# Attention, soft mixture of experts and a feed-forward layer on one core: queries and keys loaded by the batch, value tails in a home of their own

## The chip, the cores and the metric

The kernel runs on one core of one Trainium2 chip. The metric is the device time of one execution in microseconds (us); the time of a kernel is the median of several executions. Five engines each work through a list of their own: TensorE (PE, matrix products; PEld is its loading of weights), VectorE (DVE), ScalarE (ACT), GpSimd (POOL) and SyncE (SP), which here does nothing but start DMAs. Sixteen DMA engines move the data.

## What is computed

```python
def _attn_ref(q, k, v):                    # q, k, v: 8 batches, 8 heads, 576 tokens, 64 wide, float32
    scores = scale * np.matmul(q, k.transpose(0, 1, 3, 2))
    mask = block_i >= block_j              # blocks of 64 tokens
    scores = np.where(mask, scores, -1000000000.0)
    attn = np.exp(scores - max); attn = attn / (sum + 1e-09)
    return np.matmul(attn, v)
x = attn_out, one row of 512 for each of the 4608 tokens
x = _moe_ref(x, phi, w1, w2)               # soft mixture of 8 experts, 4 slots each, inner width 1024
return _moe2_ref(x, w_in, w_out)           # relu(x @ w_in) squared, @ w_out; inner width 2048
```

The three stages run one after the other. The change lies in the attention, which fills the first 435 us or so.

## The kernel before

The attention works on pairs of heads: head j and head 4 + j of one batch are a pair, so there are 8 batches of 4 pairs, 32 pairs in all, numbered n = 4b + j. `pair(n)` (L957) writes out one step: the scores of pair n, the pass over the maxima of pair n + 2 (`maxpass`, L443), the product with the values of pair n - 1 (`pv`, L583), and the splitting of queries and keys of pair n + 3 into a high and a low fp16 part (`split`, L394). PE works in exactly the order in which this is written (`manual_schedule`). SP's order is not written by hand: a scheduler puts each DMA where its own simulation finds it ready, those written earlier first, and SP then starts them strictly one after the other. A DMA whose data are not ready holds up all that stand behind it. In the program every DMA also waits for the one that was started eight places before it (eight semaphores in rotation), so at most eight are on their way.

SP starts these DMAs in the attention:

- `load_pair(n)` (L322): the keys and the queries of a pair, two heads each. `main` (L326, the DMA at L328) loads 512 tokens of one head, 128 KB; `tail` (L333, the DMA at L335), once for each batch, loads the last 64 tokens of four heads, 64 KB. They go into `qk_tile(b)` (L120): batches take turns in two places, in `ar_lo` and in `ar_hi`. `pair(n)` loads pair n + 7 (`LOOK`, L917, L1006 to L1008), so 2 + 2 of these DMAs belong to each pair, and 4 tails to each batch.
- `load_v(n)` (L301): the values of a pair, two DMAs of 128 KB (L306) and two tails of 16 KB (L312), which lie in a fifth block of the pair's own tile (`v_tile`, L124, four tiles in turn).
- the transposing DMA at L426, which turns the split keys (`ka`) into `s1`. `maxpass` needs it in the next pair. It is called s1(n) in this text, for pair n.
- the transposing DMA at L512, which turns the split queries with the maxima (`qb`) into `t2`, needed by the scores of the pair: t2(n).
- `s2copy(n)` (L924), a copy of the upper half of s1(n) into one of two tiles `s2`, needed by the second matmul of the scores (L528) of pair n, and possible once the scores of pair n - 2 are done.
- `load_in` (L908), pieces of 512 KB of w_in (`raw`), and pieces of the experts' weights w1 (L165, L167): work for the stages behind, taken in ahead.

The scales of a pair need the sum of squares of its queries and keys (`scale`, L348, the squares at L354 on ACT); this is what first reads the loaded data.

The loads stand in a list `dq`, from which four are taken at each of the eight places of a pair (`LR`):

```python
if n + LOOK < N:
    at = len(dq) if n < 1 else 0
    dq[at:at] = {0: load_pair(6), 1: load_pair(7) + load_pair(8)}.get(n) or load_pair(n + LOOK)
```

Of the kernel before, what the change touches and what calls it, by code (L numbers as in the profile page):

```python
# [23 lines left out]
def tile_attn_soft_moe_ffn(  # L24
# [12 lines left out]
    nc = tc.nc  # L37
    B, H, S, D = q.shape
# [6 lines left out]
    NJ = H // 2  # L45
    NU = S // 128
# [36 lines left out]
    ar_hi = hi_p.tile([128, NHI * 512], F32, name="ar_hi")  # L83
# [6 lines left out]
    V0 = NHI - 5  # L90
# [29 lines left out]
    def qk_tile(b):  # L120
        t = (ar_lo, ar_hi[:, 9 * 512:18 * 512])[b % 2].rearrange("p (w x j d) -> p w x j d", w=2, j=NJ, d=D)
        return dict(q=t[:, 0], k=t[:, 1])

    def v_tile(n):  # L124
        c0 = 512 * V0 + 640 * (n % 4)
        return ar_hi[:, c0:c0 + 640].rearrange("p (a h d) -> p a h d", h=2, d=D)

    def wchunk(i):
        kind, g, c = wlist[i]
# [106 lines left out]
    def attention():  # L236
# [22 lines left out]
        N = B * NJ  # L259
# [41 lines left out]
        def load_v(n):  # L301
            b, j = divmod(n, NJ)
            t = v_tile(n)

            def main(hp):
                nc.sync.dma_start(  # L306
                    out=t[:, 0:NU, hp, :], in_=v[b][NJ * hp + j, 0:128 * NU, :].rearrange("(u p) d -> p u d", p=128)
                )

            def tail():  # L310
                for h in range(2):
                    nc.sync.dma_start(out=t[64 * h:64 * h + 64, NU, 0, :], in_=v[b][NJ * h + j, 128 * NU:S, :])  # L312

            return [lambda: main(0), tail, lambda: main(1)]

        def load_phi(hp):
            nc.sync.dma_start(
# [4 lines left out]
        def load_pair(n, by={}):  # L322
            b, j = divmod(n, NJ)
            t = qk_tile(b)

            def main(nm, hp):  # L326
                src = dict(q=q, k=k)[nm][b]
                by.get(nm, nc.sync).dma_start(  # L328
                    out=t[nm][:, hp:2 * NU:2, j, :],
                    in_=src[NJ * hp + j, 0:128 * NU, :].rearrange("(u p) d -> p u d", p=128),  # L330
                )

            def tail(nm, hp):  # L333
                src = dict(q=q, k=k)[nm][b]
                by.get(nm, nc.sync).dma_start(  # L335
                    out=t[nm][64 * hp:64 * hp + 64, 2 * NU],
                    in_=src[NJ * hp:NJ * hp + NJ, 128 * NU:S, :].rearrange("j i d -> i j d"),
                )

            fs = []  # L340
            for nm in "kq":
                for f in (tail, main) if j == 0 else (main,):
                    fs += [lambda f=f, nm=nm, hp=hp: f(nm, hp) for hp in range(2)]
            return fs

        sc = {}

# [235 lines left out]
        def pv(n):  # L583
            b, j = divmod(n, NJ)
            vs = v_tile(n)
            pp = P[n]
            box = {}
# [18 lines left out]
            def tl(t):  # L606
                if t == 0:
                    box["tl"] = ps_v.tile([128, 384], F32, tag="tl", name="tl")
                for hp in range(2):
                    b_, c_ = pp[hp, 1], pp[hp, 2]  # L610
                    r = (b_[:, 0:64], b_[:, 448:512], c_[:, 256:320], c_[:, 448:512], pp["d"][:, hp, :])[t]
                    nc.tensor.matmul(
                        box["tl"][64 * hp:64 * hp + 64, 320:384], vs[:, t, hp if t < NU else 0, :], r,
                        start=(t == 0), stop=False,
                    )

# [281 lines left out]
        def wchunks(k):  # L898
            i = nxt[0]
            nxt[0] += k  # L900
            return [f for x in range(i, i + k) for f in wchunk((0, 1, 4, 5, 2, 3)[x] if x < 6 else x)]
# [12 lines left out]
            a, c = i % KD, i // KD  # L914
            return decode(dec_p, tin[:, a, 512 * c:512 * c + 512], raws.pop(i), 512)

        AHEAD, LOOK, LR = 3, 7, 4  # L917
        dq = load_pair(0, dict(q=nc.scalar)) + load_pair(1, dict(q=nc.scalar)) + load_pair(2) + load_pair(3)

        def loads(k):  # L920
# [6 lines left out]
        with tc.manual_schedule(engines={mybir.EngineType.Activation}):  # L927
            c0, c1, c2 = [scale([i]) for i in range(3)]
# [12 lines left out]
            for f in m0[6:] + m0[:6] + [sp2[0], sp2[1], sp2[3]]:  # L941
                f()
        dq += load_v(0) + load_pair(4) + load_v(1) + load_pair(5) + [lambda hp=hp: load_phi(hp) for hp in range(2)]
        s3 = scale([AHEAD])
        m1 = maxpass(1)
# [8 lines left out]
        work, aux, decq, nraw = [], [], [], [0, 0]  # L954
        NRAW = KD * FF // 512
        ew = early = late_ = last = half = None
        def pair(n):  # L957
            nonlocal dq, work, aux, decq, ew, early, late_, last, half
            bn, jn = divmod(n, NJ)
            m = maxpass(n + 2) if n + 2 < N else []  # L960
            s = scores(n) if n < N else []
# [17 lines left out]
            elif jn == 3:  # L979
                if bn + 1 == B:  # L980
                    early, late_, last = batch(bn)
# [17 lines left out]
            if n == 6:  # L999
                ew = wchunks(2)  # L1000
            if n >= 7 and ew:
                dq.append(ew.pop(0))
            if n + 2 < N:
                at = len(dq) if n < 4 else 0
                dq[at:at] = load_v(n + 2)
            if n + LOOK < N:  # L1006
                at = len(dq) if n < 1 else 0
                dq[at:at] = {0: load_pair(6), 1: load_pair(7) + load_pair(8)}.get(n) or load_pair(n + LOOK)  # L1008
            if n == 1:
                aux += scale([4]) + scale([5])  # L1010
            if n == 2:
# [40 lines left out]
            if n == N - 1:  # L1052
                half = wchunk(14)
# [595 lines left out]
```

## Time and profile before

| | |
|---|---|
| median of 3 runs | 892.95 us (890.33 to 894.09) |
| the profiled execution | 890.13 us, of which its span (first to last instruction) is 888.1 us |
| PE busy in the span | 823.8 us (93%) |
| DVE, ACT, POOL busy | 691.9 us, 627.3 us, 248.5 us |
| mean granted TensorE clock | 0.981 |
| moved by DMA | 113.18 MB in 222,022 packets, 193,760 of them under 512 B |

How to read the views used below. In a timeline a row is: start, duration (both us), engine, line, operation, output <- input, number of instructions merged; in square brackets the idle time of the engine just before, and what ended it. For SP (SPq) the duration is that of starting the DMA, with any wait in it, not that of the transfer. In the table of stretches a row is: the stretch, its length, then for PE, PEld, DVE, ACT and POOL the busy time with the number of instructions, then the granted TensorE clock (1.00 is 2.4 GHz, 0.5 is 1.2 GHz), the mean busy share of the DMA engines, and GB/s. In the table of DMA issues a row ends with KB of each and the median us from start to landing. In the chain of waits a row is: start, us, what. The waits table gives who waited for what: us in total, times, longest.

### The profile page before, as it was taken

The page shows a single profiled execution, that of the slowest core. Times are in us where ns is not written, and L with a number is a line of the kernel's source. Part 1 is how long each engine was busy: PE and PEld are TensorE (multiplying, and loading weights), DVE is VectorE, ACT ScalarE, POOL GpSimd, SP SyncE. Part 2 cuts the span into 40 slices and gives each one's busy share as a digit, 9 for nine tenths or more (in the row PEclk, how much of TensorE's full clock was granted, in tenths as well). Part 3 has the DMA queues.
Part 4 walks back from the last instruction along what each step waited for, and adds up shares of the span by engine and source line. Part 5 has one row for each costly group of instructions (what it writes and reads, how often), then busy time and mean ns, then how long its engine had stood idle before and what let it go on. Part 6 is the DMA issues. An engine that isn't in the chain of part 4 may idle for free.

```text
span 888.1 us, 21999 instructions
## 1 busy us (share of the span) xinstructions
PE 823.8 (93%) x8788; PEld 612.4 (69%) x8788; DVE 691.9 (78%) x1600; ACT 627.3 (71%) x1012; POOL 248.5 (28%) x394
## 2 busy tenths in 40 slices
PE   2778999999999999979997799999999999999997
PEld 1445767676676767656532444789898988888886
DVE  5857789999999998963633899788778888888880
ACT  5467777787878786734212889987888888887770
POOL 0225747666575756573100000000000000000000
PEclk9889999999999999999999899999999999999999
DMA  8798899999997898495999500100100000000002
GB/s 165 148 167 150 166 183 191 207 177 202 173 192 165 181 151 188 97 260 188 314 388 386 210 0 1 49 25 25 42 31 25 25 24 25 25 25 24 25 25 48
DMA packets 222022, 113.18 MB, mean 127 GB/s; under 512 B 193760, under 2 KB 195808, under 8 KB 221920
## 3 DMA queue, kind: packets, MB, share of 16 engines
q1 hardware_dynamic: 219264, 111.12, 53.3%
q8 instruction: 69, 1.13, 0.5%
q10 hardware_dynamic: 2656, 0.66, 0.4%
q14 instruction: 33, 0.27, 0.1%
HBM read 78.71 MB, written 9.44 MB: 99 GB/s over the span
## 4 chain that ended last, share of the span: by engine, by line
PE 60%; DVE 10%; DMA 8%; POOL 8%; ACT 7%; issue 3%; SPq 2%; ACTq 0%; DVEq 0%
PE ps_y L1463 14%; PE ps_x L1463 9%; PE ps_z L1463 9%; PE xm L601 5%; PE po L1485 4%; POOL ss L571 4%; PE ps_hb L1427 3%; POOL ul L711 3%; DMA wch<-in_moe_w_dram 3%; PE ps_sc L528 3%; DVE pm L465 2%; DMA s<-s 2%; DMA s<-ka 2%; PE ps_h L1154 1%; PE ps_max L451 1%
## 5 line engine op out<-in xcount | busy, mean ns | idle before, releaser
L1463 PEld LDWEIGHTS <-ah 128*128 128x128 f16 x1792 | 170.4, 98 | 21.8
L566 ACT ACTIVATE p<-ps_sc,es 128x512 f32<-128x512 f32 x192 | 128.0, 692 | 40.1 <-PE ps_sc L528 25.8
L1396 DVE TENSOR_TENSOR al<-a,ah 128x1024 f16<-128x1024 f32 (+1 forms) x128 | 138.5, 1125 | 16.7 <-ACT ah L1450 15.3
L571 POOL TENSOR_TENSOR ss<-p 128x384 f32<-128x384 f32 (+1 forms) x128 | 92.8, 745 | 171.8 <-ACT p L566 171.7
L465 DVE TENSOR_REDUCE pm<-ps_max 128x4 f32<-128x512 f32 x160 | 107.1, 681 | 32.1 <-PE ps_max L459 32.0
L1450 ACT CAST ah<-a 128x1024 f16<-128x1024 f32 (+1 forms) x128 | 114.4, 936 | 15.0 <-DVE a L1396 13.6
L528 PE MATMUL ps_sc<-t,s 128*128 128x512 f16 (+3 forms) x512 | 107.1, 302 | 12.0 <-DMA s<-s 7.9
L1556 POOL TENSOR_TENSOR ot<-u,p 128x256 f32<-128x256 f32 x16 | 12.5, 782 | 374.8 <-DVE u L1527 339.4
L1463 PE MATMUL ps_y<-bh,ah 128*128 128x256 f16 x384 | 104.8, 273 | 0.0
L1463 PE MATMUL ps_y<-bl,ah 128*128 128x256 f16 x384 | 104.7, 273 | 0.0
L1463 PE MATMUL ps_y<-bh,al 128*128 128x256 f16 x384 | 104.7, 273 | 0.0
L571 POOL TENSOR_TENSOR ss<-ss,p 128x320 f32<-128x320 f32 (+1 forms) x128 | 98.1, 766 | 10.5 <-ACT p L566 1.4
L1318 ACT ACTIVATE r<-ps_hb,alpha 128x1024 f32<-128x1024 f32 x64 | 71.1, 1112 | 34.1 <-PE ps_hb L1427 33.4
L1463 PEld LDWEIGHTS <-al 128*128 128x128 f16 x896 | 87.6, 98 | 10.0
L601 PE MATMUL xm<-p,ar_hi 128*64 128x256 f32 (+3 forms) x512 | 91.6, 457 | 0.0
L1396 DVE TENSOR_TENSOR a<-a 128x256 f32<-128x256 f32 x192 | 76.2, 424 | 3.9
L1463 PE MATMUL ps_x<-bh,ah 128*128 128x256 f16 x256 | 70.1, 274 | 0.0
L1463 PE MATMUL ps_z<-bh,ah 128*128 128x256 f16 x256 | 69.9, 273 | 0.0
L1463 PE MATMUL ps_x<-bh,al 128*128 128x256 f16 x256 | 69.8, 273 | 0.0
L1463 PE MATMUL ps_z<-bl,ah 128*128 128x256 f16 x256 | 69.8, 273 | 0.0
L1463 PE MATMUL ps_x<-bl,ah 128*128 128x256 f16 x256 | 69.8, 273 | 0.0
L1463 PE MATMUL ps_z<-bh,al 128*128 128x256 f16 x256 | 69.8, 273 | 0.0
(255 smaller groups left out, 1846.5 us busy)
## 6 DMA issues: line engine op xcount, KB each, us to landing
wch<-in_moe_w_dram SPq DMA_DIRECT2D x18, 1024.0 KB, 11.1
ar_hi<-in_v_dram SPq DMA_DIRECT2D x64, 128.0 KB, 3.2
raw<-in_moe_w_in_dram SPq DMA_DIRECT2D x16, 512.0 KB, 4.9
out_dram<-ot SPq DMA_DIRECT2D x32, 256.0 KB, 2.2
ar_hi<-in_moe_w_dram SPq DMA_DIRECT2D x6, 1024.0 KB, 8.7
s<-s SPq DMA_DIRECT2D x32, 144.0 KB, 3.4
ar_lo<-in_k_dram SPq DMA_DIRECT2D x32, 128.0 KB, 3.6
ar_hi<-in_k_dram SPq DMA_DIRECT2D x32, 128.0 KB, 3.4
```

The costliest lines, as they stand in the source:

```text
L465: nc.vector.tensor_reduce(out=o, in_=i, axis=AX.X, op=ALU.max)
L528: nc.tensor.matmul(ps[:, c0:c0 + w].rearrange("p (s c) -> p s c", c=128), kk[:, 2 * t + hp, :], qq[:, 2 * u0 + hp:8:2, :], start=(c0 == 0 ...
L566: exps[:] = [nc.scalar.activation(out=pt, in_=ps, func=AF.Exp, scale=es[:, 0:1])]
L571: add = lambda o, x, y: nc.gpsimd.tensor_tensor(out=o, in0=x, in1=y, op=ALU.add)
L601: nc.tensor.matmul(box["xm"][64 * hp:64 * hp + 64, 128 * t:512], vs[:, t, hp, :], r, start=(t == 0), stop=(t == 3),)
L711: add = lambda o, x, y: nc.gpsimd.tensor_tensor(out=o, in0=x, in1=y, op=ALU.add)
L1318: nc.scalar.activation(out=r[:, c0:c1], in_=ps[:, c0:c1], func=AF.Relu, **kw)
L1396: sub = lambda o, a, b: nc.vector.tensor_tensor(out=o, in0=a, in1=b, op=ALU.subtract)
L1427: nc.tensor.matmul(ps[:, 512 * j + 256 * a:512 * j + 256 * a + 256], ws[:, 128 * f:128 * f + 128], ctt[:, c0:c0 + 256], start=True, stop=True,
L1450: nc.scalar.copy(v(hl[n % 2][0][:, 2 * kq:2 * kq + 2], s), v(a7[n, kq], s))
L1463: nc.tensor.matmul(acc[:, 0:HM], a[:, k], b[:, k], start=bool(first and k + j == 0), stop=(k == KH - 1 and j == 2), skip_group_check=not f ...
L1485: nc.tensor.matmul(pos[t], g[:, 512 * a + 128 * t:512 * a + 128 * t + 128], tt[:, c, a], start=(c == 0 and a == 0), stop=(c == KH - 1 and ...
```

## The change

Queries and keys of the batches 2 to 7 are no longer loaded pair by pair. A new `load_batch(b)` loads a whole batch: four DMAs for the keys and four for the queries, each of 128 tokens of all eight heads (256 KB, L356 of the changed kernel), and the same four tails (L362 there). It is called in the second pair of batch b - 2: the tails and the keys are put into the list there, the queries in the pair after. Before, the four pairs of a batch were put in one by one, from the second pair of batch b - 2 on. Batches 0 and 1 are loaded as they were.

The value tails of a whole batch (64 tokens of four heads, two DMAs of 64 KB, L315 there) are loaded with the batch's first pair into a place of their own; the four value tiles shrink to four blocks.

```diff
     def v_tile(n):
-        c0 = 512 * V0 + 640 * (n % 4)
-        return ar_hi[:, c0:c0 + 640].rearrange("p (a h d) -> p a h d", h=2, d=D)
+        c0 = 512 * (V0 + n % NJ)
+        return ar_hi[:, c0:c0 + 512].rearrange("p (a h d) -> p a h d", h=2, d=D)
+
+    def v_tail(b):
+        c0 = 512 * (V0 + NJ) + 256 * (b % 2)
+        return ar_hi[:, c0:c0 + 256].rearrange("p (j d) -> p j d", d=D)
...
-            def tail():
-                for h in range(2):
-                    nc.sync.dma_start(out=t[64 * h:64 * h + 64, NU, 0, :], in_=v[b][NJ * h + j, 128 * NU:S, :])
-
-            return [lambda: main(0), tail, lambda: main(1)]
+            def tail(hp):
+                nc.sync.dma_start(
+                    out=v_tail(b)[64 * hp:64 * hp + 64],
+                    in_=v[b][NJ * hp:NJ * hp + NJ, 128 * NU:S, :].rearrange("j i d -> i j d"),
+                )
+
+            return [lambda: main(0)] + [lambda hp=hp: tail(hp) for hp in range(2) if j == 0] + [lambda: main(1)]
...
+        def load_batch(b):
+            t = qk_tile(b)
+
+            def main(nm, u):
+                nc.sync.dma_start(
+                    out=t[nm][:, 2 * u:2 * u + 2].rearrange("p x j d -> p (x j) d"),
+                    in_=dict(q=q, k=k)[nm][b][:, 128 * u:128 * u + 128, :].rearrange("h p d -> p h d"),
+                )
+
+            def tail(nm, hp):
+                nc.sync.dma_start(
+                    out=t[nm][64 * hp:64 * hp + 64, 2 * NU],
+                    in_=dict(q=q, k=k)[nm][b][NJ * hp:NJ * hp + NJ, 128 * NU:S, :].rearrange("j i d -> i j d"),
+                )
+
+            return [
+                [lambda nm=nm, hp=hp: tail(nm, hp) for nm in "kq" for hp in range(2)],
+                [lambda u=u: main("k", u) for u in range(NU)],
+                [lambda u=u: main("q", u) for u in range(NU)],
+            ]
...
-                        box["tl"][64 * hp:64 * hp + 64, 320:384], vs[:, t, hp if t < NU else 0, :], r,
+                        box["tl"][64 * hp:64 * hp + 64, 320:384], vs[:, t, hp, :] if t < NU else v_tail(b)[:, j, :], r,
...
-            if n + LOOK < N:
-                at = len(dq) if n < 1 else 0
-                dq[at:at] = {0: load_pair(6), 1: load_pair(7) + load_pair(8)}.get(n) or load_pair(n + LOOK)
+            if n == 0:
+                dq += load_pair(6)
+            if n == 1:
+                dq[0:0] = load_pair(7)
+            if jn == 1 and bn + 2 < B:
+                bl = load_batch(bn + 2)
+                dq[len(load_pair(7)) if n == 1 else 0:0] = bl.pop(0) + bl.pop(0)
+            if jn == 2 and bl:
+                dq[0:0] = bl.pop(0)
```

PE's, ACT's and POOL's instructions stay in their order, and DVE's but for some ten in the first pairs. SP's list falls from 488 entries to 392 and is ordered anew. Three places of it, all on SP; in each the first piece is the kernel before and the second the change. `s_..` with `ka` is an s1, `t_..` with `qb` a t2, `s_0` or `s_1` with `s_..` an s2copy.

The first place lies in pairs 1 and 2, from t2(2) to s1(4) (`s_648` before, `s_644` now).

```order
L512 DMA_TRANSPOSE t_634<-qb_140 128x9x128
L328 DMA ar_hi<-in_q_dram 128x4x64
L328 DMA ar_hi<-in_k_dram 128x4x64 x2
L328 DMA ar_hi<-in_q_dram 128x4x64 x2
L335 DMA ar_lo<-in_k_dram 64x4x64 x2
L328 DMA ar_lo<-in_k_dram 128x4x64 x2
L924 DMA s_0_141<-s_347 64x1152
L335 DMA ar_lo<-in_q_dram 64x4x64 x2
L328 DMA ar_lo<-in_q_dram 128x4x64
L426 DMA_TRANSPOSE s_648<-ka 128x9x128
```

```order
L539 DMA_TRANSPOSE t_631<-qb_140 128x9x128
L334 DMA ar_hi<-in_k_dram 128x4x64 x2
L334 DMA ar_hi<-in_q_dram 128x4x64 x2
L362 DMA ar_lo<-in_k_dram 64x4x64 x2
L362 DMA ar_lo<-in_q_dram 64x4x64 x2
L951 DMA s_0_141<-s_347 64x1152
L356 DMA ar_lo<-in_k_dram 128x8x64 x3
L453 DMA_TRANSPOSE s_644<-ka 128x9x128
```

Thirteen DMAs stood between the two transposes, and now twelve do, three of them of 256 KB.

The second place lies in pairs 3 to 5: s2copy(4) is `s_0_141<-s_648`, now `s_0_141<-s_644`, and s1(6) is `s_1097`, now `s_1091`; `t_1282` and `t_1270` are t2(5).

```order
L512 DMA_TRANSPOSE t_1085<-qb_139 128x9x128
L328 DMA ar_lo<-in_q_dram 128x4x64 x2
L306 DMA ar_hi<-in_v_dram 128x4x64
L426 DMA_TRANSPOSE s_1097<-ka 128x9x128
L312 DMA ar_hi<-in_v_dram 64x64 x2
L306 DMA ar_hi<-in_v_dram 128x4x64
L924 DMA s_0_141<-s_648 64x1152
L328 DMA ar_lo<-in_k_dram 128x4x64 x2
L328 DMA ar_lo<-in_q_dram 128x4x64 x2
L306 DMA ar_hi<-in_v_dram 128x4x64
L512 DMA_TRANSPOSE t_1282<-qb_140 128x9x128
```

```order
L539 DMA_TRANSPOSE t_1079<-qb_139 128x9x128
L310 DMA ar_hi<-in_v_dram 128x4x64 x2
L951 DMA s_0_141<-s_644 64x1152
L935 DMA raw<-in_moe_w_in_dram 128x1024 x2
L453 DMA_TRANSPOSE s_1091<-ka 128x9x128
L310 DMA ar_hi<-in_v_dram 128x4x64 x2
L169 DMA ar_hi<-in_moe_w_dram 128x512 x6
L951 DMA s_1_142<-s_880 64x1152
L539 DMA_TRANSPOSE t_1270<-qb_140 128x9x128
L169 DMA ar_hi<-in_moe_w_dram 128x512 x2
```

s2copy(4) moves ahead of s1(6); two pieces of w_in stand between them, and eight pieces of w1 (256 KB each) around t2(5), which before came later and one by one.

The third place recurs in every batch from batch 2 on: the pieces run from t2(11) to the copies of pairs 11 and 12 (`s_1_142` and `s_0_141`), pair 11 being the last of batch 2.

```order
L512 DMA_TRANSPOSE t_2684<-qb_140 128x9x128
L924 DMA s_1_142<-s_2249 64x1152
L328 DMA ar_lo<-in_k_dram 128x4x64 x2
L426 DMA_TRANSPOSE s_2734<-ka 128x9x128
L908 DMA raw<-in_moe_w_in_dram 128x1024
L328 DMA ar_lo<-in_q_dram 128x4x64 x2
L306 DMA ar_hi<-in_v_dram 128x4x64
L312 DMA ar_hi<-in_v_dram 64x64 x2
L306 DMA ar_hi<-in_v_dram 128x4x64
L924 DMA s_0_141<-s_2459 64x1152
```

```order
L539 DMA_TRANSPOSE t_2650<-qb_140 128x9x128
L356 DMA ar_lo<-in_q_dram 128x8x64
L310 DMA ar_hi<-in_v_dram 128x4x64
L453 DMA_TRANSPOSE s_2700<-ka 128x9x128
L315 DMA ar_hi<-in_v_dram 64x4x64
L935 DMA raw<-in_moe_w_in_dram 128x1024
L315 DMA ar_hi<-in_v_dram 64x4x64
L310 DMA ar_hi<-in_v_dram 128x4x64
L951 DMA s_1_142<-s_2223 64x1152
```

s2copy(11) came before s1(13) (`s_2734`) and now comes behind it and behind four loads.

## Rows read from the trace of the kernel before

**Rows 1.** The page, busy time of the engines.

```profile
PE 823.8 (93%) x8788; PEld 612.4 (69%) x8788; DVE 691.9 (78%) x1600; ACT 627.3 (71%) x1012; POOL 248.5 (28%) x394
```

**Rows 2.** Table of stretches: two of the attention, a short one, one of the experts.

```profile
50.00:100.00 50.00, 41.28 (x578) 27.20 (x576) 32.82 (x99) 37.20 (x77) 21.21 (x30) 0.90 0.87 158
200.00:250.00 50.00, 48.59 (x673) 34.12 (x674) 46.96 (x124) 38.10 (x79) 32.86 (x53) 1.00 1.05 189
...
48.00:54.00 6.00, 3.71 (x47) 2.48 (x46) 5.37 (x20) 5.42 (x12) 3.83 (x7) 1.00 1.15 219
...
440.00:490.00 50.00, 42.81 (x415) 14.79 (x413) 20.80 (x85) 12.95 (x24) 0.00 (x0) 0.97 1.03 377
```

**Rows 3.** Timeline of PE, 55 to 87 us: pairs 2, 3 and 4.

```profile
55.09 0.39 PE L528 MATMUL ps_sc<-t,s 128*128 128x512 f16 x1 [1.07 <-DMA s<-s]
58.21 0.59 PE L451 MATMUL ps_max<-s,t 128*128 128x128 f16 x2 [2.73 <-DMA s<-ka]
...
59.33 1.95 PE L601 MATMUL xm<-p,ar_hi 128*64 128x512 f32 x4
...
63.64 0.67 PE L435 MATMUL ps_qT<-id,qa 128*64 128x128 f16 x18
...
71.20 1.06 PE L601 MATMUL xm<-p,ar_hi 128*64 128x512 f32 x4
...
73.97 0.67 PE L435 MATMUL ps_qT<-id,qa 128*64 128x128 f16 x18
...
81.72 0.39 PE L528 MATMUL ps_sc<-t,s 128*128 128x512 f16 x1 [1.07 <-DMA s<-s]
81.94 0.38 PE L451 MATMUL ps_max<-s,t 128*128 128x128 f16 x2
...
82.58 1.60 PE L601 MATMUL xm<-p,ar_hi 128*64 128x512 f32 x4
...
87.02 0.67 PE L435 MATMUL ps_qT<-id,qa 128*64 128x128 f16 x18
```

**Rows 4.** Timeline of SP, 43 to 82 us, with one row of DVE.

```profile
43.70 1.51 SPq L512 DMA_TRANSPOSE t<-qb  x1
...
51.55 0.91 DVE L419 SCALAR_TENSOR_TENSOR ka<-ar_hi,sig,ka 128x576 f16<-128x576 f32 x1
...
54.27 1.42 SPq L426 DMA_TRANSPOSE s<-ka  x1
...
75.33 1.54 SPq L426 DMA_TRANSPOSE s<-ka  x1
...
78.83 0.51 SPq L924 DMA_DIRECT2D s<-s  x1
```

**Rows 5.** DMA issues of the whole run, by line and size.

```profile
ar_hi<-in_v_dram SPq DMA_DIRECT2D x64, 128.0 KB, 3.2
...
s<-s SPq DMA_DIRECT2D x32, 144.0 KB, 3.4
...
ar_hi<-in_v_dram SPq DMA_DIRECT2D x64, 16.0 KB, 3.3
...
s<-ka SPq DMA_TRANSPOSE x32, 4.3
```

**Rows 6.** Waits, 100 to 350 us: the longest of PE for a DMA.

```profile
PE ps_max L451 <- DMA s<-ka: 1.8, 1, 1.8
```

**Rows 7.** Timelines of SP, DVE and PE, 248 to 261 us, pair 18.

```profile
248.76 0.49 SPq L924 DMA_DIRECT2D s<-s  x1
...
252.55 0.87 DVE L419 SCALAR_TENSOR_TENSOR ka<-ar_hi,sig,ka 128x576 f16<-128x576 f32 x1
...
254.46 1.44 SPq L426 DMA_TRANSPOSE s<-ka  x1
...
260.62 0.59 PE L528 MATMUL ps_sc<-t,s 128*128 128x512 f16 x2
```

**Rows 8.** Chain of waits, 355 to 445 us: its longest step.

```profile
388.66 10.78 DMA s<-s
```

More of the change, by code (lines that the diff above doesn't have):

```diff
@@ L915, in decode_in @@
             return decode(dec_p, tin[:, a, 512 * c:512 * c + 512], raws.pop(i), 512)
-        AHEAD, LOOK, LR = 3, 7, 4
+        AHEAD, LR = 3, 4
         dq = load_pair(0, dict(q=nc.scalar)) + load_pair(1, dict(q=nc.scalar)) + load_pair(2) + load_pair(3)
@@ L956, in attention @@
         ew = early = late_ = last = half = None
+        bl = []
         def pair(n):
-            nonlocal dq, work, aux, decq, ew, early, late_, last, half
+            nonlocal dq, work, aux, decq, bl, ew, early, late_, last, half
             bn, jn = divmod(n, NJ)
```

## The prediction

> **What bounds the kernel now.** I read the page first, then the table of stretches, then the timelines of the stretches that stand out. PE is busy for 823.8 us of a span of 888.1 [rows 1], so 64 us are left, and a change of loads can only win where PE is idle or slowed. The stretches tell where that is [rows 2]. In the middle of the attention (200 to 250 us) PE is busy for 48.59 of 50 us at clock 1.00, and little is left to win. From 50 to 100 us it is busy for 41.28 us, at clock 0.90.
>
> The timeline of PE names what it waits for there [rows 3]: at 55.09 us 1.07 us for an s2copy, at 58.21 us 2.73 us for s1(4), at 81.72 us 1.07 us for s2copy(4). Each of these gaps is followed by a slow stretch: the work from the first value matmul to the transposes takes 4.31 us (59.33 to 63.64) after the first two and 4.44 us (82.58 to 87.02) after the third, against 2.77 us (71.20 to 73.97) at full clock. So the granted clock, fallen behind the gaps, costs another 1.54 and 1.67 us. All of it together, 1.07 + 2.73 + 1.07 + 1.54 + 1.67 = 8.1 us, is the most that better loads could win in the first pairs.
>
> The timeline of SP shows why two of these came late [rows 4]. The split keys of pair 4 were ready at 51.55 + 0.91 = 52.46 us, but SP started s1(4) at 54.27: it had been starting loads without a pause since t2(2) ended at 43.70 + 1.51 = 45.21, thirteen DMAs in 9.06 us, 0.70 us each. And s2copy(4) could go as soon as pair 2's scores were done, but stood behind s1(6), which was started at 75.33, and went at 78.83.
>
> **The change part by part.**
>
> *Fewer DMAs.* SP's list falls from 488 to 392 entries: 8 fewer loads of queries and keys in each of six batches, 6 fewer value tails in each of eight. At 0.70 us that is 67 us of SP's time, but SP is not on PE's path except where it is late. A tail of 16 KB lands after 3.3 us, a load of 128 KB after 3.2 [rows 5], so the small ones cost as much as the large. The Trainium skill says that transfers under 64 KB are mostly overhead and should be coalesced (DMA: Bandwidth & Descriptors, Rules for kernel authors); the rows agree. By that rule alone the sum would be nearer to the full 8.1 us. I don't take it, since the number of packets stays: each run of one head and one token is 256 B, before and after.
>
> *s1(4).* Between t2(2) and s1(4) stand twelve DMAs instead of thirteen, and ahead of t2(2) one fewer: two starts, 2 x 0.70 = 1.4 us earlier, which brings s1(4) from 54.27 to 52.9, just after its keys are ready. The twelve carry more: four loads of 128 KB, four of 64, a copy of 144 and three of 256, 1680 KB against 1424. They are started in 8.3 us, which asks for 207 GB/s; the same mix ran at 219 GB/s at 48 to 54 us [rows 2], so the queue holds. Bounds: nothing won (or 1.2 us lost, if the extra 256 KB stand in front at 219 GB/s), to 1.07 + 2.73 + 1.54 = 5.3 us if both gaps and the slow clock go. I take 1.4 us, nearest to the rows, with the slow clock left, as PE still waits over 1 us.
>
> *s2copy(4) and s1(6).* The copy now stands ahead of s1(6), so it starts at least 78.83 - 75.33 = 3.5 us earlier, and its gap of 1.07 us is gone. But two pieces of w_in, 1 MB, now stand between it and s1(6). At 377 GB/s, the rate of the long loads at 440 to 490 us [rows 2], they take 2.8 us. s1(6) was started at 75.33 and lands 4.3 us later [rows 5], at 79.6; PE asks for it at 81.94 [rows 3], and without the copy's gap at 80.9, so there is 1.3 us of room. The loads' 2.8 us use it up: PE then waits 1 to 1.5 us for s1(6) where it waited 1.07 us for the copy. I take 0, with bounds of 2.7 us won (gap and clock) and 2 us lost.
>
> *Eight pieces of w1 at once.* Six of them, 1.6 MB, stand ahead of t2(5) and s2copy(5): 4.2 us at 377 GB/s. In the kernel before these pieces came one by one. Both are needed only when pair 5 begins, and from pair 3 to pair 4 it is 11.4 us (71.20 to 82.58 [rows 3]); with 4.3 us to land, as s1 has, that leaves 2.9 us as cover, if t2(5) is ready as pair 4 begins. I take 0; without the cover up to 2 us are lost, and the clock with them.
>
> *The middle.* Each batch still moves the same bytes, with 14 fewer starts. PE waited 1.8 us in all for s1 between 100 and 350 us [rows 6]; half of it, 0.9 us, I count as won (bounds 0 and 1.8). Against that, the copy for the last pair of each batch moves behind s1 of the pair after next and four loads, 768 KB in all. In pair 18, for one: the keys are ready at 252.55 + 0.87 = 253.42 us, s1 then takes SP 1.44, the four loads 0.5 each (a copy's start took 0.49 there [rows 7]), 2.0 in all, and the copy lands 3.4 us after its start [rows 5]: 260.3 us. PE asks for it at 260.62. Before, it was started at 248.76. Its room shrinks to nothing, five times in a run (pairs 11 to 27). Bounds: 0 to 1.8 us for each time (768 KB at 219 GB/s are 3.6 us, of which SP's starts cover 2.0, and 0.2 for the room); I take 0.1, 0.5 us in all.
>
> *The end of the attention.* The copy that takes 10.78 us [rows 8], behind long loads of w1, keeps its place: 0. The value tiles' new places free no later than the old ones for the loads of w1: 0.
>
> **The sum.** 890.13 - 1.4 + 0 + 0 - 0.9 + 0.5 = 888.3 us for a run like the profiled one. The median of the runs shown lies 2.8 us above that execution; I add half of it, since a new median may lie anywhere between, and forecast **889.7 us**, about 2 us less than the kernel before on equal terms. A measurement of this kernel can tell about 0.5%, 4.5 us, from no change.
>
> **The rivals.**
>
> *The start comes free* (faster). SP's 96 fewer starts let every transpose and copy of pairs 2 to 5 go as soon as its data are ready, the three gaps close and the clock holds: 8.1 us at the start, 1.8 us in the middle less 0.5: 890.1 - 9.4 = 880.7 us; with half of the start, 885. For it: 0.70 us for each start in a stretch in which SP never paused, and gaps that all follow a late start. Against it: the loads of the start are moved earlier, 512 KB of keys more before s1(5), and w_in and w1 with them.
>
> *The copies come late* (slower). The DMAs are started in one line, and a small copy behind big loads waits for them: s2copy in rows 8 took 10.78 us instead of 3.4 [rows 5]. At the third place of SP's order the copy now has no room left, so anything over that, say 1 us for the 768 KB ahead of it in a stretch where the DMA engines' share is already 1.05 [rows 2], becomes a gap on PE in five batches, 5 us, and with the 2 us that pair 4 or 5 may lose 890.1 + 7 = 897 us. It decides from the point where the copy lands more than 7 us after the split keys are ready. The Trainium skill has the rule for it: on each DMA engine descriptors are consumed in ring order (DMA: Bandwidth & Descriptors, Queues, rings and completion order). Rows 8 agree. Against it: SP's own start times, 2.0 us for the four loads, already cover most of their transfer.
>
> *The loads themselves run faster* (faster). The new loads write 2 KB in one piece for each partition where the old ones wrote 256 B; if the write side set the rate, the start would be relieved of queue time as in the first rival: 882 us. No row shows a load whose rate tells the two sides apart.
>
> *The loads are hidden anyway* (no change). All of the terms are 0: 890 to 893 us. It is within the forecast's own range.
>
> **How the numbers follow.** The forecast, with no change as its edge: 0.45, from 885.5 to 894. The free start 0.30, of it most below 888. The late copies 0.20. Faster loads 0.05. So faster 0.35, within 0.5% 0.45, slower 0.20. Both outer cases hold much of the chance, so the range reaches from the full start, 881 us, to the late copies, 898 us; what lies beyond is at most 2 in 10.
>
> **What would show it.** In the profile of the changed kernel: s1(4) started at about 53 us and its gap on PE at 1 to 1.5 us instead of 2.73; the gap before pair 4 no longer on s2copy but on s1(6), about as long; busy PE in 50 to 100 us at 42 to 43 us; in the middle no wait for s2copy in the last pair of a batch. Wrong would be: PE idle for s2copy in pairs 11, 15, 19, 23 and 27 by more than 0.5 us each; a gap before pair 5; a clock of 1.00 from 50 to 100 us; or a change of the experts' stretch, which I count at 0.

## The result, and the profile after

The change makes the kernel slower: 904.86 us median of four executions (895.13 to 907.21) against 892.33 us of the kernel before beside it, a ratio of 1.0131 with a 95% interval of 1.009 to 1.0172. The forecast was 889.7 us with a range of 881 to 898: wrong in sign, and outside the range. The profiled execution took 904.28 us, its span 902.5 (before: 890.13 and 888.1). One execution of the runs below, 923.16 us of the run halves, was in a slower state and is left out of every number.

The page of the changed kernel, busy time of the engines (before: [rows 1]):

```profile
PE 829.6 (92%) x8788; PEld 613.8 (68%) x8788; DVE 692.9 (77%) x1600; ACT 627.9 (70%) x1012; POOL 248.4 (28%) x394
```

PE executes the same 8788 matmuls, and is busy 829.6 - 823.8 = 5.8 us longer for them. That is clock: the mean granted clock fell from 0.981 to 0.974, and 823.8 x 0.981 / 0.974 is 829.7. The span is 14.4 us longer, so the other 8.6 us are idle time. The table of stretches of the changed kernel tells where:

```profile
50.00:100.00 50.00, 37.06 (x461) 23.11 (x459) 29.71 (x90) 32.32 (x67) 19.53 (x28) 0.84 1.12 193
...
200.00:250.00 50.00, 46.51 (x643) 32.26 (x642) 44.23 (x115) 36.05 (x77) 30.13 (x47) 0.97 0.83 161
...
168.00:180.00 12.00, 8.46 (x63) 4.77 (x62) 11.76 (x29) 6.84 (x14) 7.08 (x10) 0.84 0.80 160
```

Against [rows 2], the first pairs lose 4.2 us of busy time and 2.1 us are lost from 200 to 250 us, which was full. The third row is a piece of 12 us around one gap: PE busy for 8.46 us, at a granted clock of 0.84, where the kernel before has 1.00 throughout the middle. The timeline of PE gives the gaps one by one (those over 0.6 us for a DMA, or for DVE behind one):

```profile
58.26 0.59 PE L478 MATMUL ps_max<-s,t 128*128 128x128 f16 x2 [2.56 <-DMA s<-ka]
...
72.75 0.39 PE L555 MATMUL ps_sc<-t,s 128*128 128x512 f16 x1 [2.12 <-DMA s<-s]
...
85.61 0.39 PE L478 MATMUL ps_max<-s,t 128*128 128x128 f16 x2 [0.66 <-DMA s<-ka]
...
97.72 0.59 PE L555 MATMUL ps_sc<-t,s 128*128 128x256 f16 x2 [3.96 <-DVE pm L492]
...
126.36 0.39 PE L555 MATMUL ps_sc<-t,s 128*128 128x512 f16 x1 [1.51 <-DMA s<-s]
...
176.78 0.61 PE L555 MATMUL ps_sc<-t,s 128*128 128x512 f16 x1 [2.65 <-DMA s<-s]
...
229.52 0.39 PE L555 MATMUL ps_sc<-t,s 128*128 128x512 f16 x1 [2.10 <-DMA s<-s]
...
280.40 0.39 PE L555 MATMUL ps_sc<-t,s 128*128 128x512 f16 x1 [1.90 <-DMA s<-s]
...
329.31 0.39 PE L555 MATMUL ps_sc<-t,s 128*128 128x512 f16 x1 [1.60 <-DMA s<-s]
...
352.82 0.39 PE L478 MATMUL ps_max<-s,t 128*128 128x128 f16 x2 [1.43 <-DMA s<-ka]
...
416.77 0.39 PE L555 MATMUL ps_sc<-t,s 128*128 128x512 f16 x1 [3.11 <-DMA s<-s]
```

The gap for s1(4) is as it was [rows 3]. New are the gap for s2copy(3) at 72.75, the one of 3.96 us before pair 5 at 97.72, and a row of five, at 126.36 to 329.31: they are the copies of pairs 7, 11, 15, 19 and 23, each the last pair of its batch. (Pair 27, also the last of one, has no gap over 0.3 us.) The waits of PE from 100 to 350 us sum them up:

```profile
PE ps_sc L555 <- DMA s<-s: 9.8, 5, 2.7
...
PE ps_max L478 <- DMA s<-ka: 0.9, 2, 0.5
```

In the kernel before, PE waited for the copies only once there, and 1.8 us for s1 [rows 6]:

```profile
PE ps_sc L528 <- DMA s<-s: 0.3, 1, 0.3
```

The shorter wait for s1 in this table is no gain. The 1.8 us are the wait for s1(27) at 333.49 us; in the change this wait comes at 352.82 us, 1.43 us long (the row above), just outside the stretch. With it PE waits 2.3 us for s1.

**The copy of the last pair of a batch.** SP's timeline of the changed kernel before the gap at 176.78 (pair 11):

```profile
166.57 1.78 SPq L453 DMA_TRANSPOSE s<-ka  x1
168.40 0.63 SPq L315 DMA_DIRECT2D ar_hi<-in_v_dram  x1
169.13 0.55 SPq L935 DMA_DIRECT2D raw<-in_moe_w_in_dram  x1
169.73 0.61 SPq L315 DMA_DIRECT2D ar_hi<-in_v_dram  x1
170.38 0.60 SPq L310 DMA_DIRECT2D ar_hi<-in_v_dram  x1
171.03 0.51 SPq L951 DMA_DIRECT2D s<-s  x1
```

and the step of the chain of waits that follows from its last row:

```profile
171.03 5.70 DMA s<-s
```

The copy is started 4.46 us after s1(13), behind 768 KB of loads, and lands 5.70 us after its start, at 176.73: PE goes on at 176.78. [Rows 5] have 3.4 us for this copy. By the chain of waits, the copies of pairs 15, 19 and 23 take 5.62, 5.40 and 5.03 us. Those of pairs 3 and 7 take 3.38 and 2.95, and no piece of w_in stands among the loads ahead of them: they are late by their start alone.

**The gap before pair 5.** The chain of waits of the changed kernel there:

```profile
87.39 7.99 DMA t<-qb
...
95.56 1.50 DVE qb L446
97.07 0.61 DVE pm L492
```

PE does not wait for t2(5) itself. DVE does: L446 is `low_q(8)`, which writes the low part of pair 8's queries into `qb`. There are three such tiles in turn, so pair 8 gets the one that t2(5) is still reading. Behind it on DVE stand maxima (`pm`), which must be read out of a PSUM tile before PE can go on with scores in it (maxima and scores take turns in six such tiles). And t2(5) is late for what SP starts ahead of it:

```profile
81.80 4.92 SPq L169 DMA_DIRECT2D ar_hi<-in_moe_w_dram  x6
86.82 0.47 SPq L951 DMA_DIRECT2D s<-s  x1
87.39 2.68 SPq L539 DMA_TRANSPOSE t<-qb  x1
```

Six pieces of w1 take SP 4.92 us, and the transpose, started behind them, lands after 7.99 us; the median of s1 is 4.3 [rows 5].

### The profile page after: what moved, and what is told of

It is laid out like the page before. It is cut to its first block, busy times and chain, and to the rows that moved or that the text cites. A ratio compares the mean times of both kernels' runs of the same rounds, so it can differ in the third digit from the quotient of the medians.

```text
span 902.5 us, 21854 instructions
## 1 busy us (share of the span) xinstructions
PE 829.6 (92%) x8788; PEld 613.8 (68%) x8788; DVE 692.9 (77%) x1600; ACT 627.9 (70%) x1012; POOL 248.4 (28%) x394
## 2 busy tenths in 40 slices
DMA packets 220486, 113.17 MB, mean 125 GB/s; under 512 B 192224, under 2 KB 194272, under 8 KB 220384
## 4 chain that ended last, share of the span: by engine, by line
PE 60%; DMA 12%; DVE 7%; POOL 7%; ACT 6%; SPq 4%; issue 3%; DVEq 0%; ACTq 0%
PE ps_y L1497 14%; PE ps_x L1497 9%; PE ps_z L1497 9%; PE xm L628 5%; DMA s<-s 5%; PE po L1519 4%; POOL ss L598 4%; PE ps_hb L1461 3%; PE ps_sc L555 3%; DMA s<-ka 2%; POOL ul L738 2%; DMA wch<-in_moe_w_dram 2%; PE ps_h L1188 1%; PE ps_max L478 1%; PE tl L639 1%
## 5 line engine op out<-in xcount | busy, mean ns | idle before, releaser
L555 PE MATMUL ps_sc<-t,s 128*128 128x512 f16 (+3 forms) x512 | 109.0, 306 | 24.0 <-DMA s<-s 15.0
L628 PE MATMUL xm<-p,ar_hi 128*64 128x256 f32 (+3 forms) x512 | 94.1, 467 | 0.0
```

The lines of the kernel that those rows point to most:

```text
L555: nc.tensor.matmul(ps[:, c0:c0 + w].rearrange("p (s c) -> p s c", c=128), kk[:, 2 * t + hp, :], qq[:, 2 * u0 + hp:8:2, :], start=(c0 == 0 ...
L628: nc.tensor.matmul(box["xm"][64 * hp:64 * hp + 64, 128 * t:512], vs[:, t, hp, :], r, start=(t == 0), stop=(t == 3),)
```

## The experiments

**Theory.** The loads themselves are not slower; the scheduler's order of SP's list is worse. (1) The copies of the batches' last pairs, and s2copy(3), now stand behind s1 of the pair after next and behind loads; (2) the pieces of w1, pulled ahead, stand before t2(5). **Rivals.** The size of the loads, 256 KB in one piece, keeps the small DMAs waiting wherever they stand; or the part on the value tails is at fault, not that on queries and keys.

Each run was timed against the kernel before in the same session (its medians there 891.2 to 892.3 us):

| run | median, us | ratio to before | 95% interval |
|---|---|---|---|
| halves | 907.91 | 1.0191 | 1.0152 to 1.0229 |
| (the change) | 904.86 | 1.0131 | 1.0090 to 1.0172 |
| qk_only | 898.93 | 1.0079 | 1.0049 to 1.0109 |
| held | 897.65 | 1.0077 | 1.0050 to 1.0103 |
| copy_late | 897.64 | 1.0062 | 1.0040 to 1.0083 |
| all_three | 887.42 | 0.9956 | 0.9939 to 0.9974 |
| copy_first | 887.92 | 0.9955 | 0.9934 to 0.9976 |
| keys_later | 886.98 | 0.9948 | 0.9926 to 0.9970 |
| end_only | 884.66 | 0.9929 | 0.9910 to 0.9948 |
| vtail_only | 886.22 | 0.9928 | 0.9903 to 0.9953 |
| copy_held | 884.63 | 0.9915 | 0.9895 to 0.9935 |
| vtail_end | 882.81 | 0.9900 | 0.9871 to 0.9928 |
| copy_end | 880.83 | 0.9889 | 0.9872 to 0.9906 |

### Size or order: halves

```diff
             def main(nm, u):
-                nc.sync.dma_start(
-                    out=t[nm][:, 2 * u:2 * u + 2].rearrange("p x j d -> p (x j) d"),
-                    in_=dict(q=q, k=k)[nm][b][:, 128 * u:128 * u + 128, :].rearrange("h p d -> p h d"),
-                )
+                for hp in range(2):
+                    nc.sync.dma_start(
+                        out=t[nm][:, 2 * u + hp],
+                        in_=dict(q=q, k=k)[nm][b][NJ * hp:NJ * hp + NJ, 128 * u:128 * u + 128, :].rearrange("h p d -> p h d"),
+                    )
```

> The change with each load of eight heads (256 KB) split into two of four heads (128 KB); the order of SP's list is kept, copies and w1 pieces stand where they stood. Theory (the order is at fault: the copy of a batch's last pair stands behind s1 of the pair after next and four loads, and six pieces of w1 stand ahead of t2(5)): about the time of the change, 900 to 908 us, with the gaps for the copy before pairs 11, 15, 19 and 23 still 1.5 to 3 us each. Rival (the size of the loads: 256 KB in one piece keep the copies and transposes waiting): under 897 us, with these gaps under 1 us.

Measured: 907.91 us. The timeline of PE, its gaps before pairs 3, 15 and 19:

```profile
72.55 0.39 PE L556 MATMUL ps_sc<-t,s 128*128 128x512 f16 x1 [2.68 <-DMA s<-s]
...
231.49 0.39 PE L556 MATMUL ps_sc<-t,s 128*128 128x512 f16 x1 [3.01 <-DMA s<-s]
...
284.70 0.61 PE L556 MATMUL ps_sc<-t,s 128*128 128x512 f16 x1 [4.23 <-DMA s<-s]
```

The size rival falls: with the order kept and the loads halved, all six gaps for the copies are there, 1.8 to 4.2 us each, and the time is far above the 897 us that it allowed. That they are mostly longer here can't be told from the noise: the ratios, 1.0191 and 1.0131, have intervals that overlap, and the profiled execution, 916.15 us, is a long one.

### The pieces of w1 and w_in: held

Here `t2s` is the list of the transposes t2, and `held` ties a DMA behind the latest one, in order only.

```diff
-            nc.sync.dma_start(
+            held(nc.sync.dma_start(
                 out=raw.rearrange("p f x -> p (f x)"),
...
-                dq.append(ew.pop(0))
+                dq.append(lambda f=ew.pop(0): held(f()))
```

> The change with each piece of w_in and each first piece of w1 tied in SP's list behind the latest t2, so that one piece instead of two of w_in and six of w1 stands between s2copy(4) and t2(5); the copies of the batches' last pairs stay behind s1 and the loads. Theory (two separate causes): the gap of 3.96 us at pair 5 goes, with the slow clock behind it: 4 to 7 us faster than the change, 897 to 901 us; the gaps for the copies before pairs 11, 15, 19 and 23 stay at 1.5 to 3 us. Rival (the pieces of w1 cost nothing, the lag at pair 5 is caught up later): 903 to 907 us.

Measured: 897.65 us, 4.8 us better than the change by the two ratios (1.0131 - 1.0077 = 0.54% of 892). The two intervals overlap, so the size is uncertain; that the gap goes is plain in the trace. The table of stretches of the 12 us from 84 us, in this run:

```profile
84.00:96.00 12.00, 12.00 (x186) 8.09 (x186) 11.34 (x29) 10.44 (x21) 7.35 (x12) 1.00 0.55 107
```

and in the change:

```profile
84.00:96.00 12.00, 8.98 (x132) 5.96 (x133) 6.47 (x17) 8.78 (x17) 5.95 (x9) 1.00 1.09 244
```

With one piece in place of six ahead of t2(5) PE has no gap there. The gaps for the copies of pairs 7, 11, 15, 19 and 23 stay, 1.4 to 3.9 us (its profiled execution, 906.52 us, is the longest of eleven). So the pieces ahead of t2(5) are one cause, and not the whole. The edit moves the pieces of w_in as well as those of w1, and doesn't tell them apart.

### The copies: copy_first and copy_held

```diff
+            if jn == 2 and n + 1 < N:
+                s2copy(n + 1)
             for i in range(8):
...
-                if i == 2 and n + 1 < N:
+                if i == 2 and n + 1 < N and jn != 2:
```

> The change with the copy of each batch's last pair written at the start of the pair before, so that SP's list has it ahead of s1 of the pair after next. The scheduler then also moves the first pieces of w1 from pair 5 to pairs 8 and 9. Theory: the gaps for the copy before pairs 3, 7, 11, 15, 19 and 23 (2.1, 1.5, 2.7, 2.1, 1.9 and 1.6 us in the change, 11.9 us in all) go, and the gap of 4 us at pair 5 with them: 887 to 894 us. Rival (size of the loads, or contention on the DMA engines): the waits only move to s1 or t2, over 899 us.

> The change with both edits: the copy of each batch's last pair first, and the pieces of w_in and w1 tied behind the latest t2, so that the pieces of w1 come one by one as before. Theory: like the copies first alone, 885 to 890 us, as the burst of w1 at pairs 8 and 9 there cost nothing visible; s1(4) still with a gap of 2 to 5.5 us. Rival (a burst of w1 costs wherever it stands): 3 us or more below the copies first alone, 881 to 885 us.

Measured: 887.92 us with the copies first, 884.63 us with both edits. The waits of PE with the copies first, from 45 to 350 us:

```profile
PE ps_max L478 <- DMA s<-ka: 8.8, 4, 5.5
...
PE ps_sc L555 <- DMA s<-s: 0.4, 1, 0.4
```

The 11.9 us for the copies have become 0.4. The wait for s1(4), 5.5 us, is longer than the change's 2.56; SP's list is the same in both up to there, so its order is not the reason, and what is was not settled. From held to copy_held the ratio falls by 1.0077 - 0.9915 = 1.62%, 14.4 us: the worth of the copies' place alone, more than the 9.8 us of gaps in the middle, as the gap of pair 3 and the slow clock go too. The pieces of w1 and w_in are worth 3.6 us more here (0.9955 - 0.9915), though in the run with the copies first those of w1 stood in a lump at pairs 8 and 9 and not before t2(5). The intervals of the two only just touch, so that is weak, but the time lies in the range of the rival: a lump costs something elsewhere as well.

### The place alone, in the kernel before: copy_late

```diff
-                if i == 2 and n + 1 < N:
+                if jn == 2 and 6 <= n <= 22:
+                    if i == 7:
+                        dq.insert(0, lambda: late(s2copy(n + 1)))
+                elif i == 2 and n + 1 < N:
                     dq.insert(0, lambda: s2copy(n + 1))
```

`late` ties the copy behind the latest s1 and the latest piece of w_in.

> The kernel before with one thing added: from pair 11 to pair 23, the copy of each batch's last pair (four copies) is tied in SP's list behind s1 of the pair after next and a 512 KB piece of w_in, the loads as they were. Theory (place in SP's list is what costs, whatever the loads): gaps of 1 to 3 us before pairs 11, 15, 19 and 23 and 4 to 11 us more than the kernel before: 896 to 903 us. Rival (only with the 256 KB loads does the place cost anything): 889 to 894 us.

Measured: 897.64 us, 5.5 us more than the kernel before (0.62% of 892). The waits of PE from 100 to 350 us:

```profile
PE ps_sc L538 <- DMA ar_hi<-in_v_dram: 5.4, 2, 3.1
PE ps_sc L538 <- DMA s<-s: 4.3, 2, 3.6
```

and the chain of waits at the first of them:

```profile
161.94 5.99 DMA s<-s
```

No load has changed here, and three of the four copies make gaps of 2 to 3.6 us (the fourth 0.7). The 5.4 us are put down to a load of values; SP's order has the copy just ahead of that load, and these matmuls read the copy's tile and no values. The 5.99 us for the copy are close to the 5.70 of the change. The place, behind s1 and a piece of w_in, costs by itself.

### Which half of the change: vtail_only and qk_only

vtail_only is the kernel before with `v_tail` and the tails of the change, and qk_only is the change with the values as before. Their core, against the change:

```diff
-            if n == 0:
-                dq += load_pair(6)
...
+            if n + LOOK < N:
+                at = len(dq) if n < 1 else 0
+                dq[at:at] = {0: load_pair(6), 1: load_pair(7) + load_pair(8)}.get(n) or load_pair(n + LOOK)
```

```diff
-            return [lambda: main(0)] + [lambda hp=hp: tail(hp) for hp in range(2) if j == 0] + [lambda: main(1)]
+            return [lambda: main(0), tail, lambda: main(1)]
```

> The kernel before with the part on the values alone: value tails of a batch in two DMAs with a home of their own; queries and keys loaded by the pair as before. Theory (the loads by the batch are what reorders SP's list to the copies' harm): 888 to 894 us, no gap for a copy over 1 us between 100 and 350 us. Rival (the value tails, now in one lump with a batch's first pair, are what pushes the copy back): 899 us or more, gaps before pairs 11 to 23.

> The change without its part on the values: queries and keys of batches 2 to 7 by the batch, value tails by the pair as before. In SP's list the copies of pairs 11 to 27 stand behind s1 of the pair after next and five loads, and three pieces of w1 ahead of t2(5). Theory (the loads by the batch, through the order, are the whole loss; the value tails alone made the kernel 5 us faster): 900 to 910 us, with gaps for the copy before pairs 11, 15, 19 and 23. Rival (both parts are needed for the loss): under 896 us.

Measured: 886.22 and 898.93 us. The rival on the value tails falls: alone they make the kernel 0.72% faster, 6.4 us, more than the theory had. The table of stretches of that run, and under it its waits of PE in the same stretch:

```profile
50.00:100.00 50.00, 44.77 (x627) 30.90 (x625) 36.53 (x110) 41.21 (x86) 25.60 (x40) 0.93 0.96 168
```

```profile
PE ps_max L457 <- DMA s<-ka: 1.1, 1, 1.1
PE ps_sc L534 <- DMA s<-s: 0.5, 2, 0.3
```

That is 3.5 us of busy time more than [rows 2]: the gap for s1(4) is 1.1 us instead of 2.73 [rows 3], and the two for the copies of 1.07 us nearly vanish. How much of it is the edit is less sure. The runs end_only and vtail_end below have, up to the end of the attention, the lists of the kernel before and of vtail_only. In the same stretch they show 42.25 and 43.47 us of busy time, and vtail_end waits 2.51 us for s1(4). So the tails gain 1.2 to 3.5 us there, and a shorter wait for s1(4) is not shown.

The part on queries and keys alone loses 0.79%, 7 us, and lies just under the 900 to 910 us expected. The two parts would add up to 0.07%, and the change loses 1.31%, more than the intervals allow. The chain of waits of that run at pair 11 shows where a difference lies:

```profile
166.73 4.09 DMA s<-s
```

Ahead of this copy stand tails of 2 x 16 KB, in the change of 2 x 64 KB, and there it took 5.70 us; ahead of t2(5) stand three pieces of w1 instead of six. The five gaps for the copies are 0.7 to 1.3 us. So the two parts don't add up. The traces fit tails that win where the order leaves the copies alone and cost in one lump ahead of a copy; no run moved only them.

### What is left to win: end_only, keys_later, all_three, copy_end, vtail_end

The same fault is in the kernel before at its end: the copy of [rows 8], 10.78 us, behind pieces of 1 MB. end_only writes the copy of pair 30 at the start of pair 29 there.

```diff
+            if n == 29:
+                s2copy(n + 1)
...
-                if i == 2 and n + 1 < N:
+                if i == 2 and n + 1 < N and n != 29:
```

> The kernel before with one thing changed: the copy of pair 30 is written at the start of pair 29, so that SP's list has it ahead of two pieces of 1 MB for the experts and of one more of the pieces before t2(30). Theory (place in the list is the cost there too): the copy lands 4 to 6 us after its start instead of 10.78, the gap of 5.18 us near the end of the attention goes, 886 to 889 us, 3 to 5 us under the kernel before. Rival (t2(30), or the copy of pair 31 behind the next pieces of 1 MB, takes its place): 890 to 893 us.

Measured: 884.66 us, 6.3 us less (0.71%) and more than the theory had. SP's timeline of that run:

```profile
384.57 0.49 SPq L924 DMA_DIRECT2D s<-s  x1
...
388.15 3.75 SPq L167 DMA_DIRECT2D wch<-in_moe_w_dram  x2
```

The copy now goes ahead of the two long pieces, and PE has no gap over 0.9 us for a DMA from 360 us to the end of the attention.

keys_later and all_three put batch 2's keys a pair later, on top of copy_first and of copy_held, against the gap for s1(4):

```diff
                 bl = load_batch(bn + 2)
-                dq[len(load_pair(7)) if n == 1 else 0:0] = bl.pop(0) + bl.pop(0)
+                if n > 1:
+                    dq[0:0] = bl.pop(0) + bl.pop(0)
             if jn == 2 and bl:
-                dq[0:0] = bl.pop(0)
+                dq[0:0] = sum(bl, [])
+                bl = []
```

> The change with the copies first and batch 2's tails and keys put into the list one pair later, with its queries, so that no load of 256 KB stands ahead of s1(4). Theory (the gap of 5.55 us for s1(4) in the run with the copies first is its place behind three loads of 256 KB): that gap under 1.5 us, 879 to 885 us, faster than both kernels. Rival (the bytes come anyway and only the wait moves, to s1(5), s2copy(5) or t2(5)): 886 to 890 us.

> The change with three edits: copies first, pieces of w_in and w1 behind t2, batch 2's keys a pair later. Theory (the gains of the run with copies and pieces, 884.6, and of the keys a pair later add up as far as the gap of 5.83 us for s1(4) is real): 879 to 883 us. Rival (the gap of s1(4) is made up for later, as the run with copies first and keys later was only 1 us faster than with copies first): 884 to 887 us.

Measured: 886.98 and 887.42 us; neither theory holds, and both times are those of the rivals, the second 0.4 us above its range. The timeline of PE with copies first and keys later:

```profile
54.58 0.58 PE L478 MATMUL ps_max<-s,t 128*128 128x128 f16 x2 [1.67 <-DMA s<-ka]
...
136.17 0.39 PE L478 MATMUL ps_max<-s,t 128*128 128x128 f16 x2 [2.14 <-DVE mx L525]
```

and with all three edits:

```profile
80.38 0.61 PE L562 MATMUL ps_sc<-t,s 128*128 128x512 f16 x1 [2.94 <-DMA s<-s]
```

The gap for s1(4), 5.55 us with the copies first, falls to 1.67 and 0.49, but with all three edits one of 2.94 us opens for s2copy(4). In keys_later a maximum pass at 136.17 us waits 2.14 us where it waited 1.00 with the copies first, and the copy near the end 4.02 us where it waited 3.52. The gaps over 0.3 us for a DMA or behind DVE, up to 400 us, come to 10.8 us against 12.7 with the copies first: so the wait mostly moved, and closing it won nothing that can be told in the time.

copy_end adds the end of the attention to the three edits (`if (jn == 2 or n >= 28) and n + 1 < N`), vtail_end adds the same to vtail_only (`n >= 28`).

> The three edits, and the copies of pairs 29 to 31 first as well. Theory: 3 to 4.5 us under the three edits, since the gap of 4 to 4.5 us near the end of the attention goes, 876 to 880 us. Rival: the same as with the three edits, if t2(30) is behind the long pieces in any case.

> The kernel before with the value tails of the change and the copies of pairs 29 to 31 first; queries and keys by the pair. Theory (with the copies in place, the batch loads win nothing of their own): the value tails' 5 us and the end's 6 us add up, 879 to 883 us, the same as the batch loads with all edits (880.8). Rival (the fewer and larger loads are worth something once the order is mended): 884 to 887 us.

Measured: 880.83 and 882.81 us, ratios of 0.9889 and 0.9900 to the kernel before. Both beat both kernels (copy_end lies 0.8 us above its theory, vtail_end within it), and their intervals overlap: with the copies in place, no worth of the batch loads of queries and keys over the loads by the pair can be told. copy_end has the lowest median, but is not told apart from vtail_end; two edits with the end and without the keys a pair later were not tried.

## Why the prediction was wrong

*What bounds the kernel*: right. PE is the bound, and every microsecond lost shows as a gap of PE or a slower clock behind one.

*Fewer DMAs* (not on the path, the full 8.1 us not taken): half wrong. The value tails alone won 6.4 us, of which 1.2 to 3.5 us of busy time show in the first pairs; where the rest came from is not settled. The Trainium skill's rule that small transfers are to be coalesced (DMA: Bandwidth & Descriptors, Rules for kernel authors) is borne out by that run. The packets stayed, as the working said: 222,022 before and 220,486 after, 1536 fewer, which is 16 for each of the 96 DMAs saved. What the change lost it lost at small DMAs that now stood behind larger pieces.

*s1(4)* (1.4 us won): its start came at 53.33 instead of 54.27, 0.9 us earlier, but its gap is 2.56 us against 2.73: 0.2 us won. SP's timeline of the changed kernel:

```profile
53.33 2.27 SPq L453 DMA_TRANSPOSE s<-ka  x1
...
61.24 4.85 SPq L356 DMA_DIRECT2D ar_lo<-in_q_dram  x4
...
69.33 0.51 SPq L951 DMA_DIRECT2D s<-s  x1
```

Starting the transpose took SP 2.27 us instead of 1.42, so the earlier start was no earlier landing: PE went on at 58.26 us, before at 58.21. Two kernels with one list differ by more than this 0.2 us in the same gap (1.11 and 2.51 us, vtail_only and vtail_end).

*s2copy(4) and s1(6)* (0): right. The gap for the copy is gone, and one for s1(6) in its place at 85.61, of 0.66 us where 1 to 1.5 were expected. But the step left out the copy of the pair before: four query loads, 1 MB, take SP 4.85 us ahead of s2copy(3), started at 69.33, and PE stands still for 2.12 us. No term had it.

*Eight pieces of w1 at once* (0, up to 2): the first step that failed. The cover of 2.9 us was counted up to the scores of pair 5, which read what t2(5) writes. But the tile that t2(5) reads has someone waiting for it as well: the write of pair 8's queries, which DVE ran at 90.00 us in the kernel before, 3 us ahead of pair 5's first value matmul at 93.21, with maxima queued behind it. And t2(5) landed after 7.99 us, where the working gave it 4.3. The price was 3.96 us of gap, some 4.8 us by the run held.

*The middle* (0.9 won, 0.5 lost): the step that decided. The 0.9 us for s1 were not won: 1.8 us of waits became 2.3. The copy was mis-sized: 0.1 us each in five batches, at most 1.8. Measured were 1.5 to 2.7 us, 9.8 us in five (pairs 7 to 23, not 11 to 27), and 14.4 us with the gap of pair 3 and the clock. The working had the right place and the right list, but three of its numbers came from other places in the list: s1's start 1.44 us (1.78 here), the four loads 0.5 us each (2.6 us in all, from 168.40 to 171.03), and the copy's landing after 3.4 us (5.70). Together 1.0 us more to start and 2.3 us more to land, against a room of 0.3; the gap is 2.65. The landing was taken from a median over all places, when the question was the landing behind these 768 KB; the forecast let SP's start times pay for their transfer, and they paid for only a part of it. That is the rule which stood beside the slower rival: the Trainium skill has descriptors consumed in ring order on each DMA engine (DMA: Bandwidth & Descriptors, Queues, rings and completion order). The 5.70 and 5.99 us agree. They don't show which bytes ahead count: the copy of pair 3 stood behind 1 MB of queries and landed after 3.38 us, and no run took the piece of w_in alone from ahead of a copy.

*The end* (0): as far as can be told, right. The gap there is 3.11 us against 5.18, but held, with the same two long pieces ahead of the copy, has 5.18 as well.

*The sum and the chances.* The rival "the copies come late" was the mechanism, with its place and its point of decision; it got 897 us, too little by half, and a chance of 0.20. At pair 11 the copy landed 10.2 us after its split keys were ready (166.54 to 176.73), past the 7 us named there. In ratios, the copies cost 14.4 us, the pieces ahead of t2(5) 4.8, and what is left, the run with both edits, wins 7.6 us against the kernel before. These are three steps of one chain of runs, so that they come to the 11.7 us measured (1.31% of 892) is no test. Of the 7.6 us the value tails win 6.4 by themselves. "The start comes free" did not come about: with both edits the gap for s1(4) is 5.83 us, and PE is busy for 41.30 us from 50 to 100, as before. The signs that would prove the forecast wrong were the ones that came: PE idle for the copies of pairs 11, 15, 19 and 23, though not 27, by more than 0.5 us, and a gap before pair 5.

## What to carry to other kernels

When loads are merged or moved, look in the new list for what now stands ahead of each small, late-bound DMA, and price its landing behind those very bytes, not by its median; then ask who else waits for the buffer it reads, not only who reads its result. Tie such small DMAs ahead by hand (a line or two here) before judging the loads: the same change was 1.3% slower than the kernel before as it stood, and 0.9% faster with its copies and weight pieces put in order, most of which the value tails win alone. Where a wait is closed, time the kernel, since twice here the time stayed. And don't read the worth of an edit from one gap of one trace: run it with a kernel whose list is the same there.

## What the runs showed that was not expected

- Starting a transpose takes SP anything from 1.24 to 4.74 us in the attention of both kernels, with any wait in it. 2.27 us behind three loads of 256 KB and 2.68 us behind six pieces of w1 are within that, so they are not shown to be the loads' doing.
- With the order kept, loads of 128 KB in place of 256 KB were not faster, 1.0191 against 1.0131 with intervals that overlap; the eight of them ahead of s2copy(3) took SP 5.30 us where four took 4.85.
- Not every gap cost clock. In the 12 us from the ends of the gaps of 2.10 to 3.96 us in the change (pairs 3, 5, 11 and 15) the granted clock was 0.74 to 0.86; from those of 1.51, 1.60 and 1.90 us (pairs 7, 23 and 19) it was 1.00. The length of the gap alone is no measure of it: in the kernel before, a gap of 1.07 us at 81.72 us has a slow stretch behind it [rows 3].
- Single gaps change from one execution to the next. The kernel before and end_only start the same DMAs in the same order up to 379 us, yet end_only waits here for an s1 that the kernel before has in time:

```profile
228.98 0.39 PE L451 MATMUL ps_max<-s,t 128*128 128x128 f16 x2 [2.29 <-DMA s<-ka]
```

The gaps for the copies of pairs 7 to 23 are no such chance: all five stand in the traces of the change, halves, held and qk_only, 0.7 to 4.2 us each. In the kernel before and in every run with these copies in their old place or first, none is longer than 0.32 us.
